# Strassen's scheme for the projections of the second of two feed-forward layers

## The chip, the cores and the metric

The kernel runs on one NeuronCore of one Trainium2 chip. The metric is the time of one execution on the device in microseconds (us). The engines are named as the profile names them: PE (TensorE, matmuls; PEld its weight loads), DVE (VectorE), ACT (ScalarE), POOL (GpSimd) and SP, which issues most of the DMAs.

## What is computed

Attention over a causal window of 64 positions (4 batches, 8 heads, 576 positions, 64 wide) gives x, 2304 tokens of 512. Two feed-forward layers follow, all in float32:

```python
h = x @ w_in                    # 512 -> 2048
r = np.maximum(h, 0.0)
x = (r * r) @ w_out             # 2048 -> 512
a = x @ w_a                     # 512 -> 1536
b = x @ w_b                     # 512 -> 1536
out = (a * b) @ w_out2          # 1536 -> 512
```

## The kernel before

Every float32 operand of a matmul is kept as a high and a low part (F32R), and every product is three matmuls into one PSUM bank: high by high, high by low, low by high. Tokens come in four blocks of 512 and one of 256 (BLOCKS); x lies in SBUF, transposed, as xh and xl per block. The feed-forward width comes in units of 128: 16 in the first layer, 12 in the second. For a unit and a block of the second layer (unit2), TensorE makes the projection a (4 chunks of the 512 features by 3 matmuls, into ps_a), ScalarE copies it to r, TensorE makes b (ps_b), VectorE multiplies g = r * b, ScalarE rounds g to hi, VectorE takes the remainder lo, and TensorE adds the unit's part of the output into accumulators acc, one bank for each row of 128 tokens, 3 matmuls of 512 columns each.

The weights of all units don't fit. So the units of each layer go in two groups (G1, G2); a group runs over all blocks, and its partial sums go to DRAM (part1, part2) and come back when the second group adds to them. Weights come from DRAM as float64 words and are decoded to float32 by ScalarE (c_high, c_low) and VectorE (c_sign, c_shift, c_sum), and then split (c_hi, c_lo) into one of 20 slots (N_A + N_B).

The order of all work is made when the program is built: every step is added to a Plan with its engine, cost, dependences and a rank, and the Plan places steps on each engine by the time at which they would be ready. Engines then run their queues in that order and wait for each other by semaphores.

Of the kernel before, what the change touches and what calls it, by code (L numbers as in the profile page):

```python
# [29 lines left out]
G2 = [range(0, 6), range(6, 12)]  # L30
# [4 lines left out]
N_A, N_B = 14, 6  # L35
# [7 lines left out]
class Plan:  # L43
# [15 lines left out]
    def issue(self):  # L59
# [18 lines left out]
        while len(order) < n:  # L78
# [43 lines left out]
def kernel(  # L122
# [36 lines left out]
    pools = {"ev": att.enter_context(tc.tile_pool(name="ev_s", bufs=3)), "cv": [cv_p]}  # L159
# [6 lines left out]
    plan = Plan({"w": 4, "ev": 3, "pr": 7})  # L166
# [16 lines left out]
    for ph, us in [(1, G1[0]), (1, G1[1]), (2, G2[0]), (2, G2[1])]:  # L183
        seq += [(kind, u) for u in us for kind in (("in", "out") if ph == 1 else ("a", "b", "out2"))]
# [53 lines left out]
    by_cv = {0: [], 1: []}  # L238

    def conv(key, rank):  # L240
        i = num[key]
        f = lambda g: (lambda: g(i))
        b = i - RAW
        raw_free = [("high", b), ("low", b), ("sign", b)] if b >= 0 else []
        users = by_cv[cv_pool(i)]
        cv_free = ("wlo", users[-2]) if len(users) > 1 else None
        s_free = ("sum", users[-2]) if len(users) > 1 else None
        users.append(i)
        shut = "close" if i >= N_A else None
        add(("ld", i), "SP", 0.6, f(c_load), raw_free, rank - 1, size=0.52)  # L250
        add(("high", i), "ACT", 0.58, f(c_high), [("ld", i), cv_free, shut], rank)
        add(("low", i), "ACT", 0.65, f(c_low), [("ld", i), cv_free, s_free, shut], rank)
        add(("sign", i), "DVE", 0.35, f(c_sign), [("ld", i), cv_free, s_free, shut], rank)
# [441 lines left out]
    def conv_ahead(r):  # L695
        if todo_conv:
            tiles(*todo_conv.pop(0), r)
# [110 lines left out]
```

## Time and profile before

| what | value |
|---|---|
| timed runs, median (lowest, highest) | 925.8 us (925.76, 926.7) |
| span of the profiled execution, first to last instruction | 924.3 us |
| PE busy | 908.0 us, 98% of the span |
| DVE, ACT busy | 442.3 us (48%), 383.5 us (41%) |
| moved by DMA | 86.00 MB, 93 GB/s over the span |

The profile is of one execution; its own time beside the span was not kept, so the span is compared with the median of the timed runs, 1.5 us longer. Busy time is the time in which an engine had an instruction in work; matmuls are pipelined and overlap in it. The second layer begins at about 480 us, where the first copies from ps_a stand.

### The profile page before, as it was taken

The numbers are of one execution on the slowest core, as the hardware profiler recorded it, in microseconds if no ns is written. First come the engines' busy times: TensorE is split into PE (matmuls) and PEld (weight loads), VectorE is DVE, ScalarE is ACT, GpSimd is POOL, SyncE is SP. The second block draws the span as 40 slices with busy tenths as digits, with TensorE's granted clock in tenths as the row PEclk, the third lists the DMA queues.
The fourth block names the chain that finished last, engine by engine and source line by source line (L and its number), as shares of the span: only waits on it lengthen the run. The fifth ranks groups of instructions, "written<-read, shape, count | busy, mean of one in ns | idle before, by whom it ended". The sixth has DMA issues, their size and how long they took to land.

```text
span 924.3 us, 13498 instructions
## 1 busy us (share of the span) xinstructions
PE 908.0 (98%) x5398; PEld 761.5 (82%) x5398; DVE 442.3 (48%) x850; ACT 383.5 (41%) x882; POOL 3.6 (0%) x17
## 2 busy tenths in 40 slices
PE   6899999999999999999999999999999999999998
PEld 4788888888988888888998888888898888888887
DVE  6988847568884424242598212212178121212122
ACT  6998636568773323232487211111176111111111
POOL 1000000000000000000000000000000000000000
PEclk9999999999999999999999999999999999999999
DMA  9866616315563101000164100101045020202011
GB/s 316 288 205 222 216 42 196 102 46 163 193 218 122 46 1 46 0 12 1 44 198 169 68 2 1 45 1 46 1 154 188 1 91 1 91 1 91 0 50 42
DMA packets 43102, 86.00 MB, mean 93 GB/s; under 512 B 3616, under 2 KB 14240, under 8 KB 43040
## 3 DMA queue, kind: packets, MB, share of 16 engines
q1 hardware_dynamic: 42224, 84.69, 27.7%
q8 instruction: 42, 0.69, 0.3%
q10 hardware_dynamic: 816, 0.46, 0.2%
q14 instruction: 20, 0.16, 0.1%
HBM read 70.98 MB, written 14.16 MB: 92 GB/s over the span
## 4 chain that ended last, share of the span: by engine, by line
PE 94%; ACT 3%; DMA 1%; DVE 1%; issue 0%; SPq 0%; DVEq 0%; ACTq 0%
PE acc L171 12%; PE acc L172 12%; PE acc L173 12%; PE ps_in L171 7%; PE ps_in L173 6%; PE ps_in L172 6%; PE ps_a L172 5%; PE ps_b L172 5%; PE ps_b L173 5%; PE ps_a L173 5%; PE ps_b L171 5%; PE ps_a L171 5%; PE ps_s L310 2%; PE ps_o L372 2%; PE ps_p L359 1%; ACT p L337 1%
## 5 line engine op out<-in xcount | busy, mean ns | idle before, releaser
L606 DVE TENSOR_TENSOR g<-r,ps_b 128x512 f32<-128x512 f32 (+1 forms) x60 | 38.0, 634 | 249.9 <-PE ps_b L173 248.1
L610 ACT CAST hi<-g 128x512 fp32r<-128x512 f32 (+1 forms) x60 | 34.6, 577 | 251.0 <-DVE g L606 250.7
L171 PE MATMUL ps_in<-xh,wh 128*128 128x512 f32 (+1 forms) x292 | 107.8, 369 | 0.0
L171 PE MATMUL acc<-hi,wh 128*128 128x512 f32 (+1 forms) x292 | 107.8, 369 | 0.0
L172 PE MATMUL acc<-lo,wh 128*128 128x512 f32 (+1 forms) x292 | 107.1, 367 | 0.0
L173 PE MATMUL ps_in<-xh,wl 128*128 128x512 f32 (+1 forms) x292 | 107.0, 366 | 0.0
L172 PE MATMUL ps_in<-xl,wh 128*128 128x512 f32 (+1 forms) x292 | 106.9, 366 | 0.0
L173 PE MATMUL acc<-hi,wl 128*128 128x512 f32 (+1 forms) x292 | 106.9, 366 | 0.0
L172 PE MATMUL ps_a<-xl,wh 128*128 128x512 f32 (+1 forms) x240 | 88.3, 368 | 0.0
L172 PE MATMUL ps_b<-xl,wh 128*128 128x512 f32 (+1 forms) x240 | 88.3, 368 | 0.0
L171 PE MATMUL ps_b<-xh,wh 128*128 128x512 f32 (+1 forms) x240 | 88.3, 368 | 0.0
L173 PE MATMUL ps_a<-xh,wl 128*128 128x512 f32 (+1 forms) x240 | 88.3, 368 | 0.0
L173 PE MATMUL ps_b<-xh,wl 128*128 128x512 f32 (+1 forms) x240 | 88.3, 368 | 0.0
L171 PE MATMUL ps_a<-xh,wh 128*128 128x512 f32 (+1 forms) x240 | 88.3, 368 | 0.0
L171 PE MATMUL acc<-wh,hi 128*128 128x512 f32 x216 | 84.2, 390 | 0.0
L172 PE MATMUL acc<-wl,hi 128*128 128x512 f32 x216 | 84.2, 390 | 0.0
L173 PE MATMUL acc<-wh,lo 128*128 128x512 f32 x216 | 84.0, 389 | 0.0
L472 DVE TENSOR_TENSOR g<-r 128x512 f32<-128x512 f32 (+1 forms) x73 | 46.0, 631 | 75.2 <-ACT r L465 74.9
L480 DVE TENSOR_TENSOR lo<-g,hi 128x512 fp32r<-128x512 f32 (+1 forms) x83 | 51.3, 618 | 60.5 <-ACT hi L476 58.9
L465 ACT ACTIVATE r<-ps_in 128x512 f32<-128x512 f32 (+1 forms) x83 | 44.7, 539 | 83.1 <-PE ps_in L173 82.1
L476 ACT ACTIVATE hi<-r 128x512 fp32r<-128x512 f32 (+1 forms) x83 | 47.9, 577 | 71.8 <-PE acc L173 71.1
L171 PEld LDWEIGHTS acc<-hi,wh 128*128 128x128 f32 x292 | 55.1, 189 | 9.2 <-issue 0.3
(80 smaller groups left out, 1559.9 us busy)
## 6 DMA issues: line engine op xcount, KB each, us to landing
raw<-in_w_out_dram SPq DMA_DIRECT2D x28, 512.0 KB, 4.0
q_sb<-in_qbd_dram SPq DMA_DIRECT2D x18, 512.0 KB, 6.3
part<-ev SPq DMA_DIRECT2D x34, 256.0 KB, 2.6
pr<-part SPq DMA_DIRECT2D x34, 256.0 KB, 4.2
raw<-in_w_in_dram SPq DMA_DIRECT2D x16, 512.0 KB, 3.7
v_sb<-in_vwin_dram SPq DMA_DIRECT2D x14, 512.0 KB, 3.9
k_sb<-in_kT_dram SPq DMA_DIRECT2D x17, 384.0 KB, 5.0
raw<-in_w_a_dram SPq DMA_DIRECT2D x12, 512.0 KB, 3.8
```

The source lines that it names most:

```text
L171: nc.tensor.matmul(ps, ah, bh, start=first, stop=False)
L172: nc.tensor.matmul(ps, ah, bl, start=False, stop=False)
L173: nc.tensor.matmul(ps, al, bh, start=False, stop=last)
L310: nc.tensor.matmul(T["s", c, j][e * W:(e + 1) * W, hp, :], T["q", c][r, e, hp, r], T["k", c][r, hp, e * W:e * W + P], start=not on_pe, sto ...
L337: nc.scalar.activation(out=T["p", c, j][:, hp, :], in_=T["s", c, j][:, hp, :], func=AF.Exp, bias=T["nm", c, j][:, hp:hp + 1], scale=SCALE, ...
L372: nc.tensor.matmul(ps[j * W:(j + 1) * W, hp, o], T["v", c][:, e, h * D:(h + 1) * D], T["pT", c, j][:, hp, o], start=True, stop=True,)
L465: nc.scalar.activation(out=T["r", k], in_=T["H", k], func=AF.Relu)
L472: nc.vector.tensor_tensor(out=T["g", k], in0=T["r", k], in1=T["r", k], op=ALU.mult)
L476: nc.scalar.activation(out=T["hi", k], in_=T["r", k], func=AF.Square)
L480: nc.vector.tensor_tensor(out=T["lo", k], in0=T["g", k], in1=T["hi", k].bitcast(F32), op=ALU.subtract)
L606: nc.vector.tensor_tensor(out=T["g", k], in0=T["r", k], in1=T["B", k], op=ALU.mult)
L610: nc.scalar.copy(out=T["hi", k], in_=T["g", k])
```

## The change

Units of the second layer go in pairs, and tokens in pairs of blocks of 384 (HB; three pairs). For a pair of units and a pair of blocks (a visit) the projection a is a product of 2 x 2 blocks: two units by two halves of the 512 features, times two halves of the features by two token blocks. In place of 8 products of blocks, each of 2 chunks by 3 matmuls of 384 columns, 7 are made, by Strassen's scheme in Winograd's form. A quad is these 7 products for a, or for b (function quad):

- The 7 weight operands are sums and differences of the decoded weights (conv_pair, VectorE), split into high and low again. The 7 x operands of each pair of token blocks (prepare) are made at the end of the first layer, split, and stored in DRAM (xops); load_x brings them back into 7 or 8 slots that take the place of x in SBUF, each time that the pair of blocks changes.
- The products are issued in the order 0, 2, 1, 3, 6, 4, 5 and share PSUM banks: 0, 3, 4 and 5 add into X, 1 is in Y, 2 and 6 add into Z. Between the products ScalarE copies X after 0, Z after 2 and X after 3, and VectorE adds Y, Z after 6, and X after 4 to these copies. So product 3 waits for the copy of X, 6 for that of Z, 4 for the second of X, and 5 for the addition of X.
- The second layer has three groups of four units in place of two of six, so part2 is stored and loaded once more. ROUTE goes over the token pairs forwards and backwards in turn, so that the pair stays the same when the group changes.
- The second group of the first layer runs over six blocks of 384 in place of BLOCKS.
- N_B falls from 6 to 4; the slots are shared out anew to the 256-column operands, with six more in the space of the stage buffer (claim, not shown).

The cut diff (the end of the file and the new functions on which the time depends):

```diff
-G2 = [range(0, 6), range(6, 12)]
+HB = 384
+HALVES = [(b * HB, HB) for b in range(NT // HB)]
+NPAIR = NT // (2 * HB)
+XA = 1536
+NU2 = FF2 // P
+G2 = [range(0, 4), range(4, 8), range(8, 12)]
+ROUTE = [(g, p) for g in range(len(G2)) for p in (range(NPAIR) if g % 2 == 0 else reversed(range(NPAIR)))]
 START = "i0 p0 p1 a0 p2 p3 o0 a1 b0 i1 a2 o1 i2 b1 p4 o2 i3 o3 b2 i4 o4 p5 f3 i5 f4 o5 i6 p6 f5 p7 f6 o6"
 MASK_PE = 5
...
-N_A, N_B = 14, 6
+N_A, N_B = 14, 4
...
-                ready[j] = max(ready[j], end + self.steps[j][9])
+                seen = t + cost if key[0] in ("Q", "O2") and self.steps[j][1] == "PE" else end
+                ready[j] = max(ready[j], seen + self.steps[j][9])
...
+    xops = [[dram.tile([P, 2, 2, HB], F32, name=f"xop{p}_{o}") for o in range(7)] for p in range(NPAIR)]
...
+    def prepare(p, rank):
+
+        low, high = slice(0, 2), slice(2, 4)
+        where = {0: (0, low), 1: (0, high), 2: (0, low), 4: (1, low), 3: (1, high), 5: (0, high), 6: (1, high)}
+
+        def view(o):
+            s, m = where[o]
+            return bt()[:, s, m, :]
+
+        def minus(o, x, y):
+            add(("pt", p, o), "DVE", 0.89,
+                lambda: nc.vector.tensor_tensor(out=view(o), in0=view(x), in1=view(y), op=ALU.subtract),
+                deps.pop(o), rank)
...
+            def hi():
+                nc.scalar.copy(out=buf()[:, 0], in_=view(o))
+
+            def lo():
+                nc.vector.tensor_tensor(out=buf()[:, 1], in0=view(o), in1=buf()[:, 0].bitcast(F32), op=ALU.subtract)
+
+            def st():
+                nc.sync.dma_start(out=xops[p][o], in_=buf().bitcast(F32))
+
+            add(("phi", p, o), "ACT", 0.75, hi, [*source[o], *free], r)
+            add(("plo", p, o), "DVE", 0.89, lo, [("phi", p, o)], r)
+            add(("pst", p, o), "SP", 0.6, st, [("plo", p, o)], r, size=0.79)
...
+        parts(0, rank - 3)
+        parts(1, rank - 3)
+        parts(6, rank)
+        minus(2, 4, 0)
+        minus(4, 6, 4)
+        minus(3, 6, 2)
+        minus(5, 1, 3)
+        for o in (2, 4, 3, 5):
+            parts(o, rank)
+
+    OPS = range(7)
+    ORDER = (0, 2, 1, 3, 6, 4, 5)
+    BANK = "XYZXXXZ"
+    SIDE = {0: 0, 1: 1, 2: 0, 3: 1}
+    UNIT = {0: 0, 1: 1, 2: 1, 3: 0}
...
+            def comb(o, x, y, op, deps):
+                add(key("cs", o), "DVE", c,
+                    lambda: nc.vector.tensor_tensor(out=at[o](), in0=x(), in1=y(), op=op), deps, r)
+
+            comb(2, at[4], at[5], ALU.add, [("sum", i2), *old])
+            comb(3, at[2], at[0], ALU.subtract, [key("cs", 2), ("sum", i1)])
+            comb(6, at[1], at[3], ALU.subtract, [key("cs", 3)])
+            comb(4, at[0], at[4], ALU.subtract, [key("cs", 2), key("cs", 3)])
+            made = {0: ("sum", i1), 1: ("sum", i1), 5: ("sum", i2)}
...
+            for o in OPS:
+                until = 10.0 * v + (0 if kind == "a" else 4) + 0.1 * ORDER.index(o)
+                free, tile_ = claim(until, [("Q", v, kind, o)])
+
+                def hi(o=o, tile_=tile_):
+                    w = T["w", kind, g, j, o] = tile_().rearrange("p (h c) -> p h c", h=2)
+                    nc.scalar.copy(out=w[:, 0], in_=at[o]())
+
+                def lo(o=o):
+                    w = T["w", kind, g, j, o]
+                    nc.vector.tensor_tensor(out=w[:, 1], in0=at[o](), in1=w[:, 0].bitcast(F32), op=ALU.subtract)
+
+                add(key("chi", o), "ACT", act(256), hi, [made.get(o, key("cs", o)), *free], r, lag=3.0)
+                add(key("clo", o), "DVE", c, lo, [key("chi", o)], r)
...
+            for o in ORDER:
+                slot = x_count[0] % (8 if ri > 1 else 7)
+                x_count[0] = slot + 1
+                x_at[ri, o], x_key[ri, o] = slot, ("x", ri, o)
+                free = [x_last[slot]] if slot in x_last else ["xa_free"]
+                if slot == 7 and slot not in x_last:
+                    free = [("pst", NPAIR - 1, 3)]
+                x_last[slot] = ("Q", n_up * ri + n_up - 1, "b", o)
+
+                def ld(o=o, slot=slot):
+                    nc.sync.dma_start(out=xring(slot).bitcast(F32), in_=xops[p][o])
+
+                add(("x", ri, o), "SP", 0.6, ld, [("pst", p, o), *free], r, size=0.79)
...
+            def product(o):
+                bank = BANK[o]
+                if o < 3:
+                    T[bank, q] = pools["q"].tile(
+                        [P, 512], F32, tag=bank, name=f"ps_{kind}{bank}", bufs=2 if bank == "X" else 1
+                    )[:, :HB]
+                ps, w, x = T[bank, q], T["w", kind, g, j, o], xring(x_at[ri, o])
+                for c in range(2):
+                    cs = slice(c * P, (c + 1) * P)
+                    for n, (a, b) in enumerate(((0, 0), (0, 1), (1, 0))):
+                        nc.tensor.matmul(
+                            ps, w[:, a, cs], x[:, b, c], start=o < 3 and not c and not n, stop=c == 1 and n == 2,
+                            skip_group_check=True,
+                        )
+
+            order = {
+                0: ["close2", *prev("C", 2, 2), *prev("Q", 1, 4)],
+                2: [Q(0), *prev("C", 1, 3)],
+                1: [Q(2), *prev("C", 1, 0)],
+                3: [Q(1), ("cp", v, kind, 0)],
+                6: [Q(3), ("cp", v, kind, 1)],
+                4: [Q(6), ("cp", v, kind, 3)],
+                5: [Q(4), C(1)],
+            }
+            for o in ORDER:
+                add(Q(o), "PE", 6 * 0.1735, lambda o=o: product(o),
+                    [*order[o], ("clo", kind, g, j, o), x_key[ri, o]], r)
...
+            copied = {0: ("X", 0), 1: ("Z", 2), 3: ("X", 3)}
+            added = {0: ("Y", 1), 1: ("X", 4), 3: ("Z", 6)}
...
+            def copy(i):
+                nc.scalar.copy(out=c_tile(i), in_=T[copied[i][0], q])
+
+            def total(i):
+                c = T["c", v, kind, i]
+                nc.vector.tensor_tensor(out=c, in0=c, in1=T[added[i][0], q], op=ALU.add)
+
+            def copy21():
+                nc.scalar.copy(out=c_tile(2), in_=T["X", q])
+
+            def mult(i):
+                ca = T["c", v, "a", i]
+                b = T["X", q] if i == 2 else T["c", v, "b", i]
+                nc.vector.tensor_tensor(out=ca, in0=ca, in1=b, op=ALU.mult)
+
...
+            work = [(n_up * ri + j, j, i) for j in range(n_up) for i in ((0, 2) if s == 0 else (1, 3))]
...
-    for t in range(len(BLOCKS)):
+    for t in range(len(HALVES)):
         for u in G1[1]:
-            unit1(t, u, G1[1], slice(0, BLOCKS[t][1]), nxt())
-    n_units1 = len(units)
-    for gi, us in enumerate(G2):
-        for u in us:
-            conv_ahead(rank[0] - 10)
-        for t in range(len(BLOCKS)):
-            for u in us:
-                unit2(t, u, us, nxt())
+            unit1(t, u, G1[1], slice(0, HB), nxt())
+        if t == 3:
+            add("xa_free", "POOL", 0.0, lambda: None, [("H", len(units) - 1)], 0)
+    layer2()
     with tc.manual_schedule():
         plan.issue()
 
```

On TensorE, before: in the second layer the output matmuls of one unit, then the next projection (three of its twelve rows; names are output<-moving operand, stationary operand).

```order
L171 MATMUL acc_5993<-wh_5021,hi_6082 128x512
L172 MATMUL acc_5993<-wl_5022,hi_6082 128x512
L173 MATMUL acc_5993<-wh_5021,lo_6084 128x512
L171 MATMUL ps_b_6100<-xh2_93,wh_5093 128x512
L172 MATMUL ps_b_6100<-xl2_98,wh_5093 128x512
L173 MATMUL ps_b_6100<-xh2_93,wl_5094 128x512
```

And now, in the middle of the second layer (xr are the x operands, w2 the weight operands; a row is one product of six matmuls):

```order
L900 MATMUL ps_aX_7039<-xr_4742,w2_6696 128x384 x6
L900 MATMUL ps_aZ_7078<-xr_4742,w2_6712 128x384 x6
L900 MATMUL ps_aX_7039<-xr_4764,w2_6702 128x384 x6
L900 MATMUL ps_bX_7157<-xr_4764,w2_6773 128x384 x6
L900 MATMUL ps_aX_7039<-xr_4764,w2_6699 128x384 x6
L900 MATMUL ps_bZ_7174<-xr_4742,w2_6792 128x384 x6
L900 MATMUL ps_bY_7183<-xr_4742,w2_6776 128x384 x6
L900 MATMUL ps_bX_7157<-xr_4742,w2_6813 128x384 x6
L900 MATMUL ps_bZ_7174<-xr_4742,w2_6816 128x384 x6
L900 MATMUL ps_bX_7157<-xr_4764,w2_6819 128x384 x6
L188 MATMUL acc_7060<-w2_6883,xb_5768 128x512
L189 MATMUL acc_7060<-w2_6893,xb_5768 128x512
```

The products of quad a (bank X: products 3, 4 and 5) are interleaved with the first of quad b: one product of b stands between a's products 4 and 5.

On SP, before, in the second group of the second layer: stores of finished rows and loads of partial sums (part), which wait for VectorE and for earlier DMAs.

```order
L580 DMA pr<-part_1_87 128x512 [waits DMAHW5_49]
L580 DMA pr<-part_1_87 128x512 [waits DMAHW6_49]
L580 DMA pr<-part_1_87 128x512 [waits DMAHW7_49]
L580 DMA pr<-part_1_87 128x512 [waits DMAHW1_49,DMAHW0_49]
L652 DMA out_dram<-pr 128x512 [waits DVE_49]
L652 DMA out_dram<-pr 128x512 [waits DMAHW2_49,DVE_49]
L652 DMA out_dram<-pr 128x512 [waits DMAHW3_49,DVE_49]
L652 DMA out_dram<-pr 128x512 [waits DMAHW4_49,DVE_49]
```

And now, where the token pair changes in the second weight group (xop are the stored x operands):

```order
L1034 DMA pr<-part_82 128x512 [waits DMAHW1_49]
L1034 DMA pr<-part_82 128x512 [waits DMAHW4_49]
L1034 DMA pr<-part_82 128x512 [waits DMAHW6_49]
L871 DMA xr<-xop_2_85 128x1536 [waits PE_49]
L871 DMA xr<-xop_1_84 128x1536 [waits PE_49]
L871 DMA xr<-xop_3_86 128x1536 [waits PE_49]
L871 DMA xr<-xop_6_89 128x1536 [waits DMAHW7_49,PE_49]
L871 DMA xr<-xop_4_87 128x1536 [waits DMAHW0_49,PE_49]
L871 DMA xr<-xop_5_88 128x1536 [waits DMAHW1_49,PE_49]
L871 DMA xr<-xop_0_90 128x1536 [waits DMAHW2_49,PE_49]
L1041 DMA part_82<-pr 128x512 [waits DMAHW3_49,DVE_49]
L1041 DMA part_82<-pr 128x512 [waits DMAHW4_49,DVE_49]
```

Seven loads of 768 KB have come in between; each waits for TensorE to have finished with the slot that it fills, and the stores of partial sums stand behind them.

On VectorE, before, at the start of the second layer: decoding of weights (L212, L219, L224), remainders of weights (L234) and of the units (L480), and the first product with b (L606).

```order
L212 TENSOR_SCALAR s_5199<-raw_5144 128x512
L472 TENSOR_TENSOR g_5202<-r_5176 128x256
L219 TENSOR_SCALAR a_5198<-a_5198 128x512
L224 ISA a_5198<-a_5198,s_5199 128x1024
L212 TENSOR_SCALAR s_5225<-raw_5173 128x512
L234 TENSOR_TENSOR wl_5207<-a_5118,wh_5206 128x512
L219 TENSOR_SCALAR a_5224<-a_5224 128x512
L606 TENSOR_TENSOR g_5247<-r_5194,ps_b_5178 128x512
L224 ISA a_5224<-a_5224,s_5225 128x1024
L234 TENSOR_TENSOR wl_5245<-a_5150,wh_5244 128x512
```

And now, at the same place (L936 is the addition for which TensorE waits, L815 the remainders of weight operands, L562 the last sums of the first layer):

```order
L936 TENSOR_TENSOR r_5562<-r_5562,ps_aY_5537 128x384
L237 TENSOR_SCALAR a_5567<-a_5567 128x512
L815 TENSOR_TENSOR w2_5578<-a_5507,w2_5578 128x256
L815 TENSOR_TENSOR w2_5581<-sx_3833,w2_5581 128x256
L242 ISA a_5567<-a_5567,s_5568 128x1024
L815 TENSOR_TENSOR w2_5592<-sx_3833,w2_5592 128x256
L815 TENSOR_TENSOR w2_5611<-sx_3833,w2_5611 128x256
L815 TENSOR_TENSOR w2_5614<-a_5507,w2_5614 128x256
L936 TENSOR_TENSOR g_5597<-g_5597,ps_aZ_5520 128x384
L230 TENSOR_SCALAR s_5620<-raw_5529 128x512
L237 TENSOR_SCALAR a_5619<-a_5619 128x512
L562 TENSOR_TENSOR bt_3851<-acc_5242,pr_5279 128x384
```

The instructions for which TensorE waits now stand among the weights' instructions, of which there are more and shorter ones.

## Rows read from the trace of the kernel before

**Rows 1.** The head of the page: span, busy time of each engine.

```profile
span 924.3 us, 13498 instructions
PE 908.0 (98%) x5398; PEld 761.5 (82%) x5398; DVE 442.3 (48%) x850; ACT 383.5 (41%) x882; POOL 3.6 (0%) x17
```

**Rows 2.** Windows by stage: length, busy us of each engine, clock, DMA, GB/s.

```profile
core 0: us, PE busy (x) PEld busy (x) DVE busy (x) ACT busy (x) POOL busy (x), PEclk, DMA share, GB/s
0.00:5.50 5.50, 0.00 (x1) 0.10 (x1) 0.62 (x2) 2.14 (x3) 1.86 (x11) 1.00 0.60 211
5.50:20.00 14.50, 11.72 (x131) 7.11 (x134) 10.67 (x28) 10.25 (x41) 1.75 (x7) 1.00 1.06 355
20.00:60.00 40.00, 35.97 (x448) 31.42 (x449) 35.94 (x83) 38.08 (x116) 0.00 (x0) 1.00 0.84 274
...
110.00:486.00 376.00, 376.00 (x2257) 317.40 (x2250) 216.79 (x412) 185.02 (x406) 0.00 (x0) 1.00 0.28 91
486.00:902.00 416.00, 416.00 (x1933) 348.62 (x1932) 130.04 (x223) 103.73 (x182) 0.00 (x0) 1.00 0.16 56
902.00:924.30 22.30, 18.34 (x126) 16.73 (x124) 4.83 (x11) 3.12 (x8) 0.00 (x0) 0.97 0.09 33
```

**Rows 3.** The page's chain that ended last, by engine.

```profile
PE 94%; ACT 3%; DMA 1%; DVE 1%; issue 0%; SPq 0%; DVEq 0%; ACTq 0%
```

**Rows 4.** ACT's timeline, second layer, 512 tokens: start us, us, instruction, idle before.

```profile
551.08 0.59 ACT L602 COPY r<-ps_a 128x512 f32<-128x512 f32 x1 [1.36 <-PE ps_a L173]
559.24 0.59 ACT L602 COPY r<-ps_a 128x512 f32<-128x512 f32 x1 [1.36 <-PE ps_a L173]
```

**Rows 5.** TensorE's timeline, second layer, 256 tokens: start us, us, instruction.

```profile
902.98 0.19 PEld L173 LDWEIGHTS ps_a<-xh,wl 128*128 128x128 f32 x1
...
915.99 0.28 PE L171 MATMUL ps_b<-xh,wh 128*128 128x256 f32 x1
...
917.31 0.28 PE L173 MATMUL ps_b<-xh,wl 128*128 128x256 f32 x1
917.43 0.40 PE L171 MATMUL acc<-wh,hi 128*128 128x512 f32 x1
```

**Rows 6.** VectorE's timeline where weights are decoded.

```profile
685.41 0.43 DVE L219 TENSOR_SCALAR a<-a 128x512 uint32<-128x512 uint32 x1
685.74 0.48 DVE L212 TENSOR_SCALAR s<-raw 128x512 uint16<-128x512 uint16 x1
686.10 0.69 DVE L224 CUSTOM_DVE_ANT_0 a<-a,s 128x1024 uint16<-128x1024 uint16 x1
686.69 0.43 DVE L219 TENSOR_SCALAR a<-a 128x512 uint32<-128x512 uint32 x1
...
687.86 0.42 DVE L614 TENSOR_TENSOR lo<-g,hi 128x256 fp32r<-128x256 f32 x1
688.20 0.41 DVE L606 TENSOR_TENSOR g<-r,ps_b 128x256 f32<-128x256 f32 x1
688.53 0.69 DVE L234 TENSOR_TENSOR wl<-a,wh 128x512 fp32r<-128x512 f32 x1
689.13 0.42 DVE L614 TENSOR_TENSOR lo<-g,hi 128x256 fp32r<-128x256 f32 x1
```

**Rows 7.** Timelines where one engine hands over to the next.

```profile
42.93 0.45 ACT L476 ACTIVATE hi<-r 128x256 fp32r<-128x256 f32 x1
43.43 0.39 PE L489 MATMUL acc<-hi,wh 128*128 128x256 f32 x1 [1.26 <-ACT hi L476]
...
917.71 0.42 DVE L606 TENSOR_TENSOR g<-r,ps_b 128x256 f32<-128x256 f32 x1 [1.56 <-PE ps_b L173]
918.16 0.41 ACT L610 CAST hi<-g 128x256 fp32r<-128x256 f32 x1 [1.54 <-DVE g L606]
```

**Rows 8.** DMA issues (KB, median us to landing), and windows with much DMA.

```profile
raw<-in_w_a_dram SPq DMA_DIRECT2D x12, 512.0 KB, 3.8
out_dram<-pr SPq DMA_DIRECT2D x17, 256.0 KB, 2.1
...
270.00:275.00 5.00, 5.00 (x24) 4.14 (x23) 3.46 (x7) 3.19 (x6) 0.00 (x0) 1.00 0.87 335
690.00:695.00 5.00, 5.00 (x37) 4.66 (x36) 4.50 (x10) 3.69 (x8) 0.00 (x0) 1.00 0.50 169
```

More of the change, by code (lines that the diff above doesn't have):

```diff
@@ L454, in unit1 @@
         part_1 = us is G1[0]
+        b0, width = (BLOCKS if part_1 else HALVES)[t]
+        t0 = b0 + cols.start
         early = t == 0 and part_1
@@ L567, in st_ @@
             def st_(m=m):
-                nc.sync.dma_start(out=part[t][:, m, :], in_=T["ev", layer, t, m])
-            add(("ev", layer, t, m), "DVE" if m % 2 else "ACT", 0.55, ev_,
+                nc.sync.dma_start(out=part1[:, m, t0:t0 + n], in_=T["ev", 1, t, m])
+            add(("ev", 1, t, m), "DVE" if m % 2 else "ACT", 0.55, ev_,
                 [("O", k), "close" if ring == "pr" else None], rank + 1.6, take=ring)
-            add(("st", layer, t, m), "SP", 0.6, st_, [("ev", layer, t, m)], rank + 1.6, give=("ev", layer, t, m), size=0.26)
@@ new lines, in spill1, with load_part1 @@
+            add(("st", 1, t, m), "SP", 0.6, st_, [("ev", 1, t, m)], rank + 1.6, give=("ev", 1, t, m), size=0.26)
+            acc_free[0].append(("ev", 1, t, m))
+    def load_part1(t, k, rank):
+        t0, n = HALVES[t]
+        over = [j for j, (b, w) in enumerate(BLOCKS) if b < t0 + n and t0 < b + w]
+        for m in range(KC):
+            def pl_(m=m):
+                pr = T["pr", 1, t, m] = pools["pr"].tile([P, 512], F32, tag="pr", name="pr")[:, :n]
+                nc.sync.dma_start(out=pr, in_=part1[:, m, t0:t0 + n])
+            add(("pl", 1, t, m), "SP", 0.6, pl_, [*[("st", 1, j, m) for j in over], ("O", k)], rank + 2, take="pr",
+                size=0.2)
@@ new lines, in bt, with hl_buf, xring @@
+    def bt():
+        if "bt" not in T:
+            T["bt"] = pools["stage"].tile([P, 2, KC, HB], F32, tag="bt", name="bt")
+        return T["bt"]
+    hl_users = []
+    def hl_buf(p, n):
+        if p == NPAIR - 1 and n % 2:
+            return xring(7)
+        if "hl" not in T:
+            T["hl"] = pools["stage"].tile([P, 2, 2, HB], F32R, tag="hl", name="hl")
+        return T["hl"]
+    def xring(slot):
+        k, half = "hl"[slot // 4], slot % 4
+        if ("xr", k) not in T:
+            T["xr", k] = xpool.tile([P, 4, 4 * HB], F32R, tag=f"x{k}0", name="xr")
+        return T["xr", k][:, half].rearrange("p (h c n) -> p h c n", h=2, c=2)
@@ L687, in nxt @@
         return rank[0]
-    def tiles(ph, u, r):
-        for kind in ("in", "out") if ph == 1 else ("a", "b", "out2"):
-            conv((kind, u), r)
-    todo_conv = [(1, u) for u in G1[1]] + [(2, u) for u in G2[0]] + [(2, u) for u in G2[1]]
+    todo_conv = [("in", u) if kind == "in" else ("out", u) for u in G1[1] for kind in ("in", "out")]
     def conv_ahead(r):
-        if todo_conv:
-            tiles(*todo_conv.pop(0), r)
+        for _ in range(2):
+            if todo_conv:
+                conv(todo_conv.pop(0), r)
     halves = {"a": slice(0, 256), "b": slice(256, 512), "f": slice(0, 512)}
```

487 lines of the change are left out of this document (357 added, 130 removed).

## The prediction

> **What bounds the kernel now.** I read the head of the page first: TensorE is busy for 908.0 of 924.3 us [rows 1]. The windows by stage say where the rest is: 12 us are lost before 110 us, at the start and in the attention stage, and some 4 us at the end; from 110 to 902 us TensorE has no idle time at all, while VectorE is busy for 58% of it in the first layer and 31% in the second, ScalarE for 49% and 25%, and the DMA engines for 0.28 and 0.16 [rows 2]. The granted clock is 1.00 (the 2.4 GHz level) in every stage that matters. The chain that ended last agrees: 94% of it is TensorE [rows 3]. So a matmul that disappears from the second layer is time off the end, as long as the engines that feed TensorE keep up; and any wait put into that stretch is time on the end.
>
> **What a matmul costs.** A unit of the second layer on a 512-token block is 24 projection and 12 output matmuls, and the copies of its result are 8.16 us apart [rows 4]: 0.2267 us for 512 columns. Twelve matmuls of 256 columns take 917.43 - 915.99 = 1.44 us [rows 5]: 0.120 each. No row has 384 columns. The two known sizes differ by 0.1067 us for 256 columns, which is one column a cycle at 2.4 GHz, and leave 0.0133 us that is the same for both; on that line 384 columns take 0.1733 us. The bounds are 0.170 (three quarters of the 512-column time) and 0.180 (one and a half 256-column times). I take the line, because its slope is just the rate of the granted clock. The weight loads don't limit it: one takes 0.19 us [rows 5], yet 256-column matmuls start every 0.12 us beside them.
>
> The Trainium skill ("TensorE: Matmul & The Clock Gate", Back-to-back issue gap) gives N/2.4 + 2.5 ns for a warm matmul: 216, 109 and, for 384 columns, 162.5 ns. The trace is 11 ns above it at both sizes that it shows. By the page the sum of the next paragraph would be -33.8 us in place of -30.8.
>
> **The change on TensorE.** Removed are the projections of the second layer: 12 units x 24 matmuls on four blocks of 512 (1152 x 0.2267 = 261.2 us) and one of 256 (288 x 0.120 = 34.6), 295.7 us. Added are 36 quads (18 visits, for a and for b) of 7 products of 6 matmuls: 1512 x 0.1733 = 262.1 us. The output matmuls stay 648 of 512 columns. The second group of the first layer goes from blocks of 512 and 256 to six of 384: 216 x (6 x 0.1733 - 4 x 0.2267 - 0.120) = +2.9 us, since each matmul pays its fixed part and there are more of them. Net: -33.6 + 2.9 = **-30.8 us**. With 0.170 for all 2808 new matmuls it is -40.2, with 0.180 it is -12.1.
>
> **What moves to VectorE, ScalarE and DMA.** VectorE instructions back to back are 0.34 us apart at 256 elements and 0.60 at 512, so 0.47 at 384 and 0.87 at 768; the three steps of a weight's decoding are 0.36, 0.33 and 0.59 [rows 6].
>
> In the steady state a visit has 14 vector instructions of 384 and three of 512: 6.6 + 1.8 = 8.4 us beside 84 x 0.1733 + 36 x 0.2267 = 22.7 us of TensorE. That is hidden. Within a quad, though, TensorE now waits for others three times. The hardest is product 5, which adds into bank X only after VectorE has read X as product 4 left it. From the start of the last matmul of a product to VectorE's start the trace shows 0.40 us (917.31 to 917.71), from VectorE's start to the next engine's 0.45 (917.71 to 918.16), and ScalarE hands over to TensorE just as fast (0.50 for an instruction of 0.45) [rows 5, 7]. With 384 columns in place of 256 that is 0.45 + 0.58 = 1.03 us. In the new order one product of the next quad (1.04 us) stands between in eight or so of the quads, two output steps (1.36) or more in the others, so TensorE comes to product 5 at 0.17 + 1.04 = 1.21 us or later. There are 0.18 us to spare, if VectorE is free. So a steady quad costs nothing; without the product in between it would cost 0.86 us.
>
> VectorE is not free where weights are decoded. At the layer boundary, from the last sum of block 4 of the first layer to the last remainder of the second visit, 120 instructions stand in VectorE's queue (39 of 384, 37 of 256, 10 of 768, 4 of 512, ten decodings): 18.3 + 12.4 + 8.7 + 2.4 + 12.8 = 54.6 us. TensorE has 354 x 0.1733 + 24 x 0.2267 = 66.8 us of work there: 82%. At a change of weight group it is 34 x 0.335 + 29 x 0.47 + 8 x 1.28 + 2 x 0.6 = 36.4 us beside 41.4: 88%. VectorE is a queue in order, so a sum for which TensorE waits can stand behind a 0.60 us instruction; less the 0.18 to spare, that is 0.3 to 0.4 us. I put 12 quads (four at the start, four at each of two group changes) at 0.3: 3.6 us, between 0 and 10. For the boundary itself, where ScalarE and the loads of the raw weights have to keep step too, I take 2 us, between 0 and 8.
>
> The x operands: 21 stores of 768 KB go out under the first layer, where the DMA engines are at 0.28 [rows 2]. Their making is 14 us of VectorE for every 75 us of TensorE, hidden at 58% load; uncovered it would be 41 us. Seven loads of 768 KB come back at each of six changes of token pair. Each waits until the last quad has used its slot. From the end of product 2 of that quad TensorE has 13.7 us of other work (the rest of the quad, ten output steps and product 0 of the next) before it needs the second operand, and 21.0 us before it needs the last of the six that weren't loaded early. With 2.1 us for the landing of a small transfer [rows 8], 4.7 MB have to move in 19 us: 249 GB/s, or 290 with the partial sums that share the queue. The trace reaches 335 and 355 GB/s where much is queued [rows 2, 8]. So I cost these at nothing, but this is the thinnest cover of all: at 238 GB/s the whole gain would be gone.
>
> Costed at nothing too: the tail (the same sums and stores end both kernels), the fifth change of accumulators in the first layer (TensorE runs three projections ahead there), and the attention stage, where the order changes a little; 1 us either way.
>
> **The sum.** 924.3 - 30.8 + 2 + 3.6 = 899.1 us of span. The span is 1.5 us under the median of the timed runs (925.8), so: **900.6 us**.
>
> **The rivals.** (1) No stall: VectorE always comes in time, and the time is 895.0. For it: it is idle for 69% of the second layer now [rows 2]. Against: the 82 and 88% above.
>
> (2) VectorE sets the pace of the quads: product 5 finds it behind another instruction in every quad, 36 x 0.5 = 18 us, and the boundary costs its 8. That gives 925.8 - 30.8 + 26 = 921. For it: 0.18 us is little, and VectorE is busy for 4.50 of 5.00 us where weights are decoded now [rows 8]. Against: in 24 quads no weights are decoded.
>
> (3) Slower: the x operands come late. The nearest rate with weights loading is 169 GB/s [rows 8], but that queue was not full. At 214 GB/s the 5.5 MB of a change take 25.7 us in place of 19, 6.8 us late, six times: 41 us, or 925.8 - 30.8 + 5.6 + 41 = 942. It decides from 4.2 us per change on, since six of these eat the 25.2 us that are left. Against: 335 and 355 GB/s. The Trainium skill ("DMA: Bandwidth & Descriptors", Bandwidth) asks for transfers of 1 MiB for three quarters of the peak, and these have 768 KB; its table has 341 GB/s at 1 MB, which is what the trace shows with transfers of half that size.
>
> That the products are not 7 for 8 is excluded: the order has 1512 such matmuls.
>
> **How the numbers follow.** A measurement of this kernel can't tell a difference under about 0.2% (1.9 us). Forecast, 897 to 908 us: 0.58. No stall, below 897: 0.12. VectorE's pace, 908 to 924: 0.18. Within 0.2%: 0.03. Slower: 0.09. The range goes from 892 (no stall, and a somewhat cheaper 384-column matmul) to 917, which takes in the lower 0.11 of (2): 0.81. Faster 0.88, same 0.03, slower 0.09.
>
> **What would show it.** The 384-column matmuls start 0.173 us apart; at 0.180 the first term is wrong by 19 us. The second layer is about 409 us of TensorE work plus stalls. Idle time of TensorE before L900 would be released by DVE L936 in (2), by a transfer xr<-xop in (3); in the forecast it is a few us in all, around the start of the second layer and the two group changes. If the output matmuls (L188 to L190) wait, remainders or weights are late. I would be wrong above all if a wait sits in each of 36 quads or six route changes: small ones add up there.

## The result, and the profile after

The changed kernel takes 903.2 us (median of four, 901.7 to 905.0), the kernel before beside it 925.8 us: ratio 0.9754, 95% interval 0.9739 to 0.9768. The forecast was 900.6 us with a range of 892 to 917. The profiled execution took 902.28 us, 1.9 us more than its span. Timed twice more beside later experiments, it took 902.5 and 901.4 us (one execution far out of line is left out there).

The head of the page after, to be read beside [rows 1]:

```profile
span 900.4 us, 14809 instructions
PE 882.2 (98%) x5686; PEld 810.2 (90%) x5686; DVE 553.6 (61%) x1134; ACT 437.1 (49%) x1048; POOL 3.5 (0%) x17
```

TensorE has lost 26 us of busy time and is still busy for 98% of the span. VectorE has gained 111 us without becoming the bound. The windows by stage, as in [rows 2] (length, busy us of each engine, clock, DMA share, GB/s):

```profile
core 0: us, PE busy (x) PEld busy (x) DVE busy (x) ACT busy (x) POOL busy (x), PEclk, DMA share, GB/s
0.00:110.00 110.00, 96.67 (x1071) 77.02 (x1072) 90.96 (x207) 92.27 (x288) 3.55 (x17) 1.00 0.79 260
110.00:478.00 368.00, 368.00 (x2433) 344.55 (x2432) 216.56 (x418) 175.33 (x401) 0.00 (x0) 1.00 0.37 127
478.00:500.00 22.00, 21.23 (x121) 20.59 (x120) 21.17 (x53) 16.36 (x37) 0.00 (x0) 1.00 0.40 131
500.00:520.00 20.00, 20.00 (x106) 18.56 (x105) 19.70 (x36) 11.01 (x22) 0.00 (x0) 1.00 0.62 225
520.00:600.00 80.00, 80.00 (x419) 74.44 (x418) 42.28 (x93) 38.20 (x81) 0.00 (x0) 1.00 0.62 234
600.00:620.00 20.00, 20.00 (x107) 18.72 (x106) 18.31 (x44) 15.05 (x34) 0.00 (x0) 1.00 0.34 108
...
720.00:760.00 40.00, 40.00 (x214) 37.71 (x213) 35.27 (x79) 23.98 (x53) 0.00 (x0) 1.00 0.37 120
760.00:885.00 125.00, 125.00 (x659) 116.94 (x658) 52.08 (x95) 30.10 (x63) 0.00 (x0) 1.00 0.43 154
885.00:900.40 15.40, 11.34 (x51) 9.08 (x49) 5.87 (x11) 0.58 (x2) 0.00 (x0) 0.97 0.44 154
```

The place to look at is 478 to 520 us: VectorE is busy for 40.9 of 42 us there, at the layer boundary, and TensorE still idles for only 0.8 us. From 520 to 885 us VectorE is at 0.55 on the whole, and at 0.92 and 0.88 in the two stretches in which the next group's weights are made (600 to 620 and 720 to 760 us); TensorE has no idle time there. The chain that ended last [rows 3] is TensorE for 87%; DMA has come up from 1% to 4%:

```profile
PE 87%; DVE 5%; DMA 4%; ACT 3%; issue 1%; ACTq 0%; DVEq 0%; SPq 0%
```

Part of that is the end. The chain in order of time, from 889 us (start us, us, what):

```profile
889.62 3.53 DMA out_dram<-pr
...
893.21 3.63 DMA pr<-part
...
897.03 0.42 DVE pr L1038
```

The last partial sums are loaded when the store ahead has freed their buffer (there are five such buffers now, seven before), and the last sum begins at 897.03.

The waits of TensorE in the second layer, by what released them (us in total, times, longest), first of the matmuls and then of the weight loads ahead of them:

```profile
PE ps_aZ L900 <- DVE lo L936: 0.7, 1, 0.7
...
PEld ps_aZ L900 <- DVE lo L936: 1.1, 1, 1.1
PEld ps_bX L900 <- ACT lo L932: 0.5, 2, 0.4
PEld ps_bX L900 <- DVE lo L936: 0.3, 1, 0.3
```

No x operand (xr<-xop) is among the releasers. TensorE's timeline, as in [rows 5], with the beginning of the first layer's second group, of the second layer, a piece of its middle and the last matmul:

```profile
256.04 0.34 PE L188 MATMUL ps_in<-xh,wh 128*128 128x384 f32 x1
...
477.96 1.20 PE L900 MATMUL ps_aX<-xr,w 128*128 128x384 f32 x6
...
712.27 1.20 PE L900 MATMUL ps_aZ<-xr,w 128*128 128x384 f32 x6
713.31 1.20 PE L900 MATMUL ps_aX<-xr,wx 128*128 128x384 f32 x6
714.35 0.39 PE L188 MATMUL acc<-w,gp 128*128 128x512 f32 x1
...
716.43 1.23 PE L900 MATMUL ps_aX<-xr,wx 128*128 128x384 f32 x6
...
895.95 0.39 PE L190 MATMUL acc<-w,gp 128*128 128x512 f32 x1
```

Six matmuls of 384 columns take 713.31 - 712.27 = 1.04 us, 0.1733 each: the line between the two known sizes was right. The nine of 512 columns from 714.35 to 716.43 take 2.08 us, though, and not 9 x 0.2267 = 2.04. From 477.96 to the end of the last output matmul (895.95 + 0.23) it is 418.2 us. The matmuls issued in it (1512 of 384, 648 of 512, and 24 of 384 left of the first layer) need 413.1 us at 0.1733 and 0.2267; this sum I call the bare work. So TensorE ends 5.1 us behind it. I call that the delay. Followed from product to product along the timeline it shows where each part of it arises, as a jump, and it is what I compare below.

### The profile page after: what moved, and what is told of

Its sections match the earlier page's. It is cut to its first block, busy times and chain, and to the rows that moved or that the text cites. A ratio compares the mean times of both kernels' runs of the same rounds, so it can differ in the third digit from the quotient of the medians.

```text
span 900.4 us, 14809 instructions
## 1 busy us (share of the span) xinstructions
PE 882.2 (98%) x5686; PEld 810.2 (90%) x5686; DVE 553.6 (61%) x1134; ACT 437.1 (49%) x1048; POOL 3.5 (0%) x17
## 4 chain that ended last, share of the span: by engine, by line
PE 87%; DVE 5%; DMA 4%; ACT 3%; issue 1%; ACTq 0%; DVEq 0%; SPq 0%
PE acc L189 12%; PE acc L188 12%; PE acc L190 12%; PE ps_bX L900 8%; PE ps_aX L900 8%; PE ps_in L188 6%; PE ps_in L190 6%; PE ps_in L189 6%; PE ps_aZ L900 4%; PE ps_bZ L900 4%; PE ps_aY L900 2%; PE ps_bY L900 2%; PE ps_s L334 1%; PE ps_o L396 1%; PE ps_p L383 1%; DMA raw<-in_w_out_dram 1%
## 5 line engine op out<-in xcount | busy, mean ns | idle before, releaser
L188 PE MATMUL acc<-hi,wh 128*128 128x384 f32 (+2 forms) x328 | 113.7, 347 | 0.0
L188 PE MATMUL ps_in<-xh,wh 128*128 128x384 f32 (+2 forms) x328 | 113.7, 347 | 0.0
L189 PE MATMUL acc<-lo,wh 128*128 128x384 f32 (+2 forms) x328 | 113.0, 344 | 0.0
L190 PE MATMUL ps_in<-xh,wl 128*128 128x384 f32 (+2 forms) x328 | 112.9, 344 | 0.0
L189 PE MATMUL ps_in<-xl,wh 128*128 128x384 f32 (+2 forms) x328 | 112.8, 344 | 0.0
L190 PE MATMUL acc<-hi,wl 128*128 128x384 f32 (+2 forms) x328 | 112.8, 344 | 0.0
L900 PE MATMUL ps_bX<-xr,w 128*128 128x384 f32 x378 | 76.2, 336 | 0.0
L900 PE MATMUL ps_aX<-xr,w 128*128 128x384 f32 x360 | 72.4, 335 | 0.0
L190 PE MATMUL acc<-w,xb 128*128 128x512 f32 x180 | 70.9, 394 | 0.0
L189 PE MATMUL acc<-w,xb 128*128 128x512 f32 x180 | 70.8, 393 | 0.0
L188 PE MATMUL acc<-w,xb 128*128 128x512 f32 x180 | 70.0, 389 | 0.0
L900 PEld LDWEIGHTS ps_bX<-xr,w 128*128 128x128 f32 x378 | 66.6, 188 | 2.3 <-ACT lo L932 0.5
L900 PEld LDWEIGHTS ps_aX<-xr,w 128*128 128x128 f32 x360 | 63.8, 188 | 1.6
```

The source lines that it names most:

```text
L188: nc.tensor.matmul(ps, ah, bh, start=first, stop=False)
L189: nc.tensor.matmul(ps, ah, bl, start=False, stop=False)
L190: nc.tensor.matmul(ps, al, bh, start=False, stop=last)
L900: nc.tensor.matmul(ps, w[:, a, cs], x[:, b, c], start=o < 3 and not c and not n, stop=c == 1 and n == 2, skip_group_check=True,)
```

## The experiments

All were timed beside the kernel before, on the same chip; a ratio is to that kernel, with its 95% interval.

| kernel | median us | ratio (interval) | TensorE's delay in the second layer |
|---|---|---|---|
| changed kernel | 903.2 | 0.9754 (0.9739 to 0.9768) | 5.1 us |
| x_once | 901.5 | 0.9734 (0.9716 to 0.9752) | 5.0 |
| eight | 937.8 | 1.0125 (1.0106 to 1.0145) | 4.2 |
| no_gap | 913.0 | 0.9856 (0.9840 to 0.9873) | 16.7 |
| thrice_sum | 933.2 | 1.0072 (1.0056 to 1.0088) | 35.4 |
| x_half | 912.7 | 0.9853 (0.9840 to 0.9867) | 15.9 |
| x_double | 941.1 | 1.0161 (1.0146 to 1.0177) | 43.1 |
| again, again_2 | 902.5, 901.4 | 0.9745 (0.9732 to 0.9758), 0.9737 (0.9724 to 0.9751) | -, 5.6 |
| decode_later, decode_later_2 | 900.8, 901.0 | 0.9731 (0.9713 to 0.9750), 0.9729 (0.9715 to 0.9742) | 5.2, 5.5 |
| before_early | 929.3 | 1.0036 (1.0022 to 1.0050) | 0.3 |
| fewer_switches | 906.2 | 0.9783 (0.9769 to 0.9797) | 9.9 |

My theory of the result: TensorE is the bound all through, and the eighth of the projections that falls away comes off the end. The rivals: VectorE's additions, or the loads of the x operands, hold TensorE up and hide part of the gain.

**Eight products.** In product():

```diff
-                for c in range(2):
+                for c in (0, 0, 1, 1) if o == 5 else (0, 1):
```

> Changed: product 5 is made twice, so that a quad has eight products and not seven (and its result is not the reference's). Theory (TensorE is the bound throughout, so the time follows the number of products): 36 x 6 x 0.1733 = 37.4 us more, 940.6, which is some 15 us slower than the kernel before. Rival (waits hide part of the products): less than 30 us more, since the waits of the next product are covered by the added one.

Measured: 937.8 us, 34.6 more than the changed kernel (spans: 35.2 more). In the second layer the added work is 37.4 us and the delay 0.9 less, so 36.5 arrive; in the two profiles the second group of the first layer also begins 0.7 us earlier and the end is 0.6 us shorter, which gives the 35.2. The time follows the number of products. It also gives the bill for all the rest of the change: with eight products a quad the changed kernel is 1.25% slower than the kernel before.

**The x operands loaded once.** In load_x():

```diff
-            if ri and ROUTE[ri - 1][1] == p:
+            if ri:
```

> Left out: the x operands are loaded only for the first token pair, and the other two pairs are computed with the operands of the first; 33 MB of loads at the six changes of token pair fall away. Theory (the loads are hidden behind TensorE's other work): the time stays within 1 us of the changed kernel's 903.2. Rival (loads late, or their traffic slows the matmuls): TensorE is 5.1 us behind its bare work at the end of the second layer, and a part of that, 2 to 4 us, comes back: about 900.

Measured: 901.5 us, 1.7 us under 903.2 and so 0.7 beyond the theory's 1 us; but the changed kernel itself took 902.5 and 901.4 us when it was timed again, so the time doesn't decide. The delay does: 5.0 us in place of 5.1. At the first change of token pair the DMA engines moved 405 GB/s in the changed kernel and 137 GB/s here; TensorE has no idle time in either. The row of the changed kernel, then that of x_once:

```profile
520.00:540.00 20.00, 20.00 (x103) 18.29 (x102) 3.90 (x9) 7.23 (x14) 0.00 (x0) 1.00 1.00 405
```

```profile
520.00:540.00 20.00, 20.00 (x104) 18.35 (x103) 8.39 (x21) 10.63 (x22) 0.00 (x0) 1.00 0.40 137
```

The loads cost nothing, and their traffic doesn't slow the matmuls either.

**More traffic ahead of the loads**, half as much again and as much again (x_double, with x_half's copy cut in half):

```diff
                 def ld(o=o, slot=slot):
+                    if ri:
+                        dump = dram.tile([P, 2, 2, HB], F32, name=f"dump{ri}_{o}")
+                        nc.sync.dma_start(out=dump, in_=xops[p][o])
```

> Added: ahead of each of the 42 later loads of an x operand a copy of 384 KB from memory to memory on the same queue, 2.75 MB for each change of token pair. Theory (the loads are hidden with little to spare; the queue moves some 400 GB/s when full, as at 520 to 540 us of the changed kernel): 5.5 + 0.8 + 2.75 = 9.05 MB take 22.6 us where 21.0 are covered: 0 to 2 us late at each of six changes, 0 to 10 us more, 903 to 913. Rival (much to spare): no change.

> Added: the same with copies of 768 KB, 5.5 MB for each change of token pair. Theory: 11.8 MB at 400 GB/s take 29.5 us where 21.0 are covered: 8.5 us late at each of six changes, 51 us more, 954. Rival (much to spare: the loads begin early enough, or the queue is faster): under 10 us more. The two together say how far the cover of the loads reaches.

Measured: 9.5 and 37.9 us more than the changed kernel, at the upper end of the first forecast and below the second. The trace has the time at which each operand lands; set against the start of the first product that uses it, it gives the cover itself. In the changed kernel the closest operand lands 1.65 us ahead of its product at the first change of token pair and 5.3 us or more ahead at the five others; in x_half these are 0.04 us and 1.1 us or more. So the cover is thin at one change and not at all six, as both forecasts had it.

In x_half three of the six changes lose anything: the first (from 526 to 538 us, 3.6 us in jumps of the delay), the one at 723 us (4.7) and the last (2.2). At the first, products wait for x operands. The other two give way where I had not looked. At 723 us VectorE and TensorE read so (start us, us, instruction, idle before and what ended it):

```profile
721.98 0.69 DVE L1041 TENSOR_TENSOR pr<-acc,pr 128x512 f32<-128x512 f32 x1 [3.50 <-DMA pr<-part]
722.59 0.54 DVE L939 TENSOR_TENSOR r<-r,ps_aX 128x384 f32<-128x384 f32 x1
723.05 0.75 DVE L815 TENSOR_TENSOR wx<-a,wx 128x256 fp32r<-128x256 f32 x2
...
723.19 2.29 PE L903 MATMUL ps_aX<-xr,wx 128*128 128x384 f32 x6 [2.91 <-DVE r L939]
725.27 0.63 PE L188 MATMUL acc<-w,gp 128*128 128x512 f32 x1
```

The x operand is there. Late are the partial sums (pr<-part), which share the queue: VectorE waits 3.5 us for them, and the addition for product 5 stands behind in the order of the plan. Of TensorE's waits in x_half 4.9 us at X were released by such an addition, at 723 us and at the last change, and 2.5 us by an x operand. Some 1.5 us of the 4.7 is not wait: the clock is at half there (last section). In the changed kernel itself this wait doesn't reach TensorE. So 9.5 us lies in the first forecast's range partly for a reason that the forecast didn't have. In x_double 9.0 us of TensorE's waits were released by x operands and 14.2 us by partial sums or an addition behind them.

**Less between products 4 and 5.** The planner takes product 5 for ready when product 4 ends:

```diff
+            if key[0] == "Q" and key[3] == 4:
+                end = t + cost
...
+                if key[0] == "C" and key[3] == 1 and self.steps[j][0][0] == "Q" and self.steps[j][0][3] == 5:
+                    seen = t + 0.01
...
-                    [*order[o], ("clo", kind, g, j, o), x_key[ri, o]], r)
+                    [*order[o], ("clo", kind, g, j, o), x_key[ri, o]], r - 50 * (o == 5))
```

> Changed: the planner is told that product 5 is ready as soon as product 4 ends, so it puts less between them: nothing in 9 quads, one output step (0.68 us) in 15, 1.04 us or more in 12; in the changed kernel 1.04 us or more stand in all 36. The work is the same. Theory (the way from product 4 over VectorE to product 5 takes 0.86 us beyond product 4's last matmul): 9 x 0.86 + 15 x 0.18 = 10.4 us more, 913.6. Rival 1 (the handover is shorter than priced, 0.5 us): 4.5 us more, 907.7. Rival 2 (VectorE is busy with other instructions when product 4 ends, as at the layer boundary): some 0.5 us more in each of the 24, 22 us in all, 925.

Measured: 913.0 us, 9.8 more. One of the nine quads with nothing in the gap:

```profile
886.02 1.21 PE L904 MATMUL ps_aX<-xr,w 128*128 128x384 f32 x6
887.27 0.55 DVE L940 TENSOR_TENSOR r<-r,ps_aX 128x384 f32<-128x384 f32 x1 [0.42 <-PE ps_aX L904]
887.87 1.33 PE L904 MATMUL ps_aX<-xr,w 128*128 128x384 f32 x6 [0.65 <-DVE r L940]
889.04 1.21 PE L904 MATMUL ps_bX<-xr,w 128*128 128x384 f32 x6
```

Product 4 would have let product 5 begin at 886.02 + 1.04 = 887.06; it begins 0.81 us later at 887.87. (In the delay, which also counts what the six matmuls lost beside it, these quads show 0.92 to 0.95.) Those with one output step between lose 0.13: a way of 0.68 + 0.13 = 0.81. Priced were 0.86. So with one product in between, 1.04 us, there is 1.04 - 0.81 = 0.23 us to spare; the prediction had 0.18. New is the row after the wait: product 5 takes 889.04 - 887.87 = 1.17 us in place of 1.04.

**A longer chain.** In total():

```diff
-                nc.vector.tensor_tensor(out=c, in0=c, in1=T[added[i][0], q], op=ALU.add)
+                for _ in range(3 if i == 1 else 1):
+                    nc.vector.tensor_tensor(out=c, in0=c, in1=T[added[i][0], q], op=ALU.add)
```

> Changed: VectorE adds bank X after product 4 three times in place of once (the result is not the reference's); the order of the work is the same, each of the 36 chains from product 4 to product 5 is two instructions of 0.47 us longer, and VectorE has 34 us more to do. Theory: the chain needs 1.80 us beyond product 4's last matmul; 9 quads have 1.04 us of other work there (0.76 short), 18 have 1.36 (0.44 short), two 1.72, the others more: 6.8 + 7.9 + 0.2 = 15 us more, 918. Rival (VectorE has slack that covers it, because product 5 comes later than the order says): under 5 us more. Rival (VectorE paces the quads already): all of the 34 us, 937.

Measured: 933.2 us, 30 more: twice the forecast, and near the rival in size. The rows tell the two apart:

```profile
829.60 1.73 DVE L937 TENSOR_TENSOR r<-r,ps_aX 128x384 f32<-128x384 f32 x3 [0.42 <-PE ps_aX L900]
...
831.38 1.31 PE L900 MATMUL ps_aX<-xr,w 128*128 128x384 f32 x6 [0.43 <-DVE r L937]
```

VectorE was idle for 0.42 us before the three additions, so it doesn't pace the quads; the chain does. Three take 1.73 us: each needs the one before, and two more cost 1.18 us, where I had priced 0.94 from instructions that don't depend on each other. The stalls in the delay are 0.95 us in the quads with 1.04 us between and mostly 0.62 with 1.36: 1.04 + 0.95 = 1.99 and 1.36 + 0.62 = 1.98, one and the same chain. To each stall come 0.11 to 0.13 us in the product behind it. So the chain without the two more additions is 1.99 - 1.18 = 0.81 us, as in no_gap. The layer boundary, where VectorE has no slack, loses 5 us in place of 1.3.

**The decoding of two weights.** The second layer accounted for, TensorE was still 2.0 us late on entering the second group of the first layer: 256.04 us, where the kernel before has 254.00. The new conv() had dropped a dependence: the weights of that group were decoded when the attention stage was over, and two of them now go ahead. decode_later puts it back in the changed kernel, before_early takes it out of the kernel before:

```diff
+        shut = "close" if N_A <= i < n_single else None
...
-        add(("high", i), "ACT", 0.58, f(c_high), [("ld", i), *cv_free], rank)
+        add(("high", i), "ACT", 0.58, f(c_high), [("ld", i), *cv_free, shut], rank)
```

(the same for c_low and c_sign; before_early has "close" from N_A + 2 on in place of N_A).

> Changed: the weights of the first layer's second group wait with their decoding for the end of the attention stage, as in the kernel before (the change let two of them be decoded earlier). The order of TensorE's work in the first 160 stretches is then that of the kernel before. Theory (the early decoding takes VectorE and ScalarE away from the attention stage, where they are at 0.9, and costs the 2.0 us by which the second group begins later): the second group begins at 254.0, and the time is 2 us lower than the changed kernel's on the same chip, 901.2. Rival (the 2.0 us are scatter between executions): no difference beyond 0.5 us.

> The changed kernel once more, beside the next one on the same chip, as its yardstick: 903 us; its first layer's second group begins between 255.4 and 257.1 us in the five profiles so far that have its attention stage (254.0 in the kernel before).

> The changed kernel, as the yardstick of the three others on this chip: 902 to 903 us; its first layer's second group begins at 255.4 to 257.1 us.

> The later decoding once more, since 900.79 against 902.5 us was within the scatter of the executions. Theory (early decoding costs the attention stage 2 us): 1.5 to 2.5 us below the changed kernel, and the second group begins at 253.4 to 254.1 us. Rival (scatter): no difference beyond 0.5 us.

> The kernel before, with this one part of the change: the decoding of two weights of the second group no longer waits for the end of the attention stage. TensorE's order in the first 160 stretches is then that of the changed kernel. Theory: 1.5 to 2.5 us more than the kernel before, 927.7, and the second group begins at 255.4 to 257.1 us in place of 254.0. Rival (something else in the change delays the attention stage, or scatter): no difference, 925.8.

The second group's first matmul in decode_later, then in before_early:

```profile
253.53 0.34 PE L188 MATMUL ps_in<-xh,wh 128*128 128x384 f32 x1
```

```profile
256.91 0.40 PE L171 MATMUL ps_in<-xh,wh 128*128 128x512 f32 x1
```

The profiles sort themselves by this one dependence: 253.5 (here), 254.1 (decode_later_2) and 254.7 us (fewer_switches) with it, 255.4 to 257.1 in the eight profiles of the changed kernel and its other variants without. They also show where the time goes. TensorE's order is the same in all eleven up to 84 us, and on the mean of either kind it gets there within 0.1 us of the same time. Then come 408 matmuls of which 256 stand in other places, and at the first one behind them it is 125.0 us with the dependence and 127.0 without. The two weights are decoded at 83 and 100 us in the changed kernel, at 210 us in decode_later. Whether the 2.0 us come from VectorE and ScalarE being taken up or from TensorE's other order isn't separated. before_early is slower than the kernel before by 3.2 us, interval 2.0 to 4.6. So the edit costs the attention stage some 2 us. What it gives back in the changed kernel is less sure by the clock: 1.7 us beside the first repeat (900.8 against 902.5), 0.4 beside the second (901.0 against 901.4), and executions of one kernel lie 1 to 5 us apart. decode_later has the lowest medians of all, but isn't shown to beat the changed kernel in time.

**Fewer changes of matmul size.** Three output steps of a unit as one of nine matmuls, except in the last block, with the later decoding:

```diff
                     def step(v=v, i=i, u=u, m=m, first=first, last=last):
+                        for m in range(3) if not final and m == 2 else (m,) if final else ():
...
-                    rr = base + 10 * v + 5 if s == 0 else r_end + 9 + m + 0.1 * n
+                    rr = base + 10 * v + 5 if s == 0 else r_end + 9 + (m if final else 0) + 0.1 * n
-                    add(("O2", ri, s, j, d, m), "PE", 3 * 0.227, step, deps, rr)
+                    add(("O2", ri, s, j, d, m), "PE", 3 * 0.227 if final else 9 * 0.227 * (m == 2), step, deps, rr)
```

> Later decoding, and the three output steps of a unit (one for each accumulator) made as one step of nine matmuls, except in the last block; TensorE then goes from 384-column to 512-column matmuls 43 times in the second layer in place of 69. Theory (each such change costs 0.04 us, the first nine 512-column matmuls taking 2.08 us in place of 2.04): 1.0 us less delay in the second layer than the 5.1 us of the changed kernel, some 899.8 us. Rival (the longer steps delay products for which VectorE waits, or accumulators come free later): stalls of 0.1 us and more take the place, no gain or a loss of 1 to 3 us.

Measured: 906.2 us, the rival. Two jumps of 2.0 us stand at 615 and 755 us, where the next group's weights are made, and there ScalarE comes late with a copy:

```profile
614.57 0.51 ACT L975 CAST xb<-g 128x384 fp32r<-128x384 f32 x1
614.99 0.47 ACT L933 COPY r<-ps_aX 128x384 f32<-128x384 f32 x1
...
615.51 1.31 PE L901 MATMUL ps_aX<-xr,wx 128*128 128x384 f32 x6 [1.45 <-ACT r L933]
```

Another 1.4 us go at the layer boundary, from 507 to 515 us. And the gain isn't there: the 512-column stretches, waits left out, lose 1.6 us in all with it, 2.1 without, 0.5 less and not 1.0. The reading "0.04 us for each change" was wrong. In the changed kernel a stretch of three loses 0.02 us, of six 0.03, of nine or more 0.04: the first nine matmuls are slower, whichever way they are grouped.

## Why the prediction was right, point by point

- **The projections, -33.6, and the first layer's second group, +2.9**: right. The 384-column matmul is 0.1733 us. The second group needs 216 x 6 x 0.1733 = 224.6 us and 1.4 us of an earlier block; by the first L900 at 477.96, with 4.2 us of it left, 221.9 us had passed since 256.04, which is 224.6 + 1.4 - 4.2 to within 0.1. By the formula for a warm matmul in the Trainium skill ("TensorE: Matmul & The Clock Gate", Back-to-back issue gap), which it calls the gap of a single, isolated one, an estimate for 384 columns is 162.5 ns; the trace is 11 ns above it at this size too.
- **Twelve quads that wait in the decoding, 3.6**: the step was right in kind and mis-sized. One quad waited, at 635.76, for VectorE's addition: 0.17 us, and 0.12 in the product behind. VectorE was as busy there as forecast (0.92 and 0.88 above), and yet in the other quads it was free, or early enough, when its addition was due: taking the busy share for a wait in each of twelve quads was the error.
- **The boundary, 2**: 1.3 us, from 494 to 499 us. The first 0.3 is ScalarE's copy of X (L932). The larger part, 0.9 and 0.1 behind it, is not product 5 but bank Z, a wait from one quad to the next, where the prediction had waits within a quad alone: the next quad's product 2 waits for VectorE to have read Z, and this addition stood behind three instructions of a weight's decoding.

```profile
495.53 0.47 DVE L230 TENSOR_SCALAR s<-raw 128x512 uint16<-128x512 uint16 x1
495.88 0.43 DVE L237 TENSOR_SCALAR a<-a 128x512 uint32<-128x512 uint32 x1
495.95 1.20 PE L900 MATMUL ps_aX<-xr,w 128*128 128x384 f32 x6
496.22 0.55 DVE L936 TENSOR_TENSOR hi<-hi,ps_bY 128x384 f32<-128x384 f32 x1
496.68 0.68 DVE L242 CUSTOM_DVE_ANT_0 a<-a,s 128x1024 uint16<-128x1024 uint16 x1
497.29 0.55 DVE L936 TENSOR_TENSOR lo<-lo,ps_bZ 128x384 f32<-128x384 f32 x1
...
497.88 0.61 PE L900 MATMUL ps_aZ<-xr,w 128*128 128x384 f32 x2 [0.73 <-DVE lo L936]
```

- **The spare time of 0.18 us at product 5**: right (no_gap: 0.23), and with it the zero for the steady quad.
- **The x loads at nothing, "the thinnest cover of all"**: right that they cost nothing (x_once); thin only at the first of the six changes, where 1.65 us are left, against 5.3 or more at the others. The 13.7 us for the second operand don't follow from their own parts (five products, ten output steps and product 0 are 13.0), but nothing else hangs on them. I had feared 238 GB/s; the queue moved 402 GB/s over the 24 us in which it was full:

```profile
515.00:539.00 24.00, 24.00 (x122) 21.69 (x121) 8.79 (x17) 8.39 (x17) 0.00 (x0) 1.00 1.01 402
```

These are transfers of 768 KB and less. The Trainium skill ("DMA: Bandwidth & Descriptors", Bandwidth) has 341 GB/s at 1 MB, for transfers that GpSimd issues. Here many transfers are in flight at once, and the trace is above it.

- **The attention stage, "1 us either way"**: the step that failed. It is 2.0 us late, since I read the order of the second layer closely and passed over a dependence that left conv() (decode_later, before_early).
- **The tail, at nothing**: the last sum begins 897.03 - 895.95 = 1.08 us after the last matmul, behind the load shown above; the handover alone is 0.40 [rows 5, 7]. The rest of the end is shorter, so that from the last matmul's start to the end of the span it is 4.45 us, 4.30 in the kernel before.
- **Not priced**: the 512-column matmuls behind 384-column ones, 2.1 us over 68 stretches; and 1.4 us in amounts under 0.15 over some 250 products, whose cause I can't name.

The sum was 899.1 and is 900.4: stalls 4.0 less, the attention stage 2.0 more, the matmuls 3.5 more, which leaves 0.2 us open. The errors nearly cancel, so that the forecast came within 2.6 us of 903.2 is in part luck; that TensorE is the bound and that the missing products come off the end is not (eight). Rival (1), no stall, had the waits right to 1.6 us but not its 895. Rivals (2) and (3) are ruled out by the waits of TensorE above, and by x_once for the third.

## What to carry to other kernels

On a kernel that TensorE bounds from one end to the other, price a change by the matmuls that it adds and drops, at start-to-start times from the trace, and then ask of every new wait how much other work stands between its two ends: here 1.04 us against a way of 0.81, and taking the work away cost 10 us. A queue's wait spreads: a late load stopped VectorE, and so an addition that had nothing to do with it, and so TensorE. And read the whole diff for dependences that vanish: a step that may go earlier will, and here that cost 2 us in a stage that the change was not about.

## What the runs showed of the hardware

- In no_gap a product that follows a wait of TensorE takes 0.11 to 0.14 us more than its six matmuls need (1.17 in place of 1.04 us at 887.87), with the granted clock at 1.00: a stall costs its length and this. Why is open.
- After a wait of 2.91 us (x_half, 723.19) six matmuls took 725.27 - 723.19 = 2.08 us, twice their 1.04, and the granted clock was 0.50 for them, the 1.2 GHz level; after waits of 2.02 us (x_half, 863.74) and 1.45 us (fewer_switches) it was 1.00, and they took 1.16 and 1.15. In x_double it was 0.50 after waits of 2.06, 2.69, 6.03 and 8.19 us, and six matmuls took 2.05 to 2.09 us. So a late operand can cost more than its lateness. The row of the stretch at 723.19 us:

```profile
723.19:725.27 2.08, 2.08 (x6) 2.08 (x7) 2.08 (x6) 0.69 (x1) 0.00 (x0) 0.50 0.36 135
```

- The first nine 512-column matmuls after 384-column ones take 0.04 us more than nine further on in the same stretch, in the changed kernel and in x_once, which has less DMA traffic, alike. What makes them slower is open.
